# One load of w3 is issued as five: 96 partitions and four times 8 partitions

## The chip, the cores and the metric

The kernel runs on one core of one Trainium2 chip. The metric is device time in microseconds (us): the median of three runs is 822.88 us before the change, and the three lie between 820.26 and 823.59 us.

The core has five engines, each with an instruction stream of its own that it works through in order: PE (matrix multiplication, with its weight loads shown as PEld), DVE (VectorE), ACT (ScalarE), POOL (GpSimd) and SP (SyncE). In this kernel SP issues the DMA transfers. Engines wait for one another, and for transfers, on semaphores.

## The reference, cut to what matters

Three parts follow one another: attention with a window of 128 positions, a gated product layer, and a layer with a squared ReLU.

```python
scores = scale * np.matmul(q, k.transpose(0, 1, 3, 2))      # 4 x 8 heads, 576 x 64
scores = np.where(mask, scores + bias[None], -1000000000.0) # 0 <= rel < 128
attn = softmax(scores)
x = np.matmul(attn, v)                                      # -> 2304 x 512
h = (x @ w1) * (x @ w2) @ w3                                # w3: 1024 x 1024
x = h @ w_out                                               # 1024 x 512
h = np.maximum(x @ w_in, 0.0)
out = h * h @ w_out2
```

The weights come as 64-bit floating point numbers. The kernel reads them as pairs of 32-bit words and makes 32-bit numbers of them on ACT and DVE.

## The kernel before, in words

**Stages.** The first 150 us or so are attention, worked in 16 pairs of heads. For a pair, two loads (L393, one a head, 64 partitions each) bring q and k into one tile `qk`, of which there are two; four loads (L398, L402, L406, L407) bring v. PE makes the scores (L467) from `qk`, DVE adds the bias and takes a minimum (L435), ACT takes the exponential (L443), PE transposes (L503), ACT or DVE copies the transposes (`pt`, L200), and PE multiplies with v (L527, L543). The first 64 rows of `qk` belong to the pair's first head and the last 64 to its second, so the first matmul of a pair needs the first of its two loads, and the second matmul needs the second one.

**What lies between.** In the gaps of attention the kernel loads weights and multiplies w3 by w_out (L659), which is needed from the first product layer on. w3 comes in 8 blocks, `("w3", 0)` to `("w3", 7)`, each of 128 partitions x 8192 bytes, by `w_load`; w_out comes in 4 such blocks, also by `w_load`. Each block is then made into 32-bit numbers by three instructions: `conv_s` (L339 when on DVE), `conv_g` (ACT, L330) and `conv_m` (DVE, L345). The later stages (L195 to L197, L1080 to L1082, L1131 to L1133) are long rows of matmuls.

**What sets the order.** The class `Plan` simulates the engines with a cost for each task and writes one fixed order for each engine's instructions before the kernel is built. A load task such as `ldw30` has one cost, whatever number of DMA instructions `w_load` issues for it. SP issues all loads and stores in the planned order, one after the other, and an issue that waits holds up all that stand behind it.

**Eight semaphores for the transfers.** The framework gives the transfers eight semaphores in turn, DMAHW0 to DMAHW7. From the ninth transfer on, each issue first waits until the transfer that had the same semaphore, the eighth before it, has landed. Beside that an issue waits for the engine that still reads the tile it will overwrite.

The function `w_load` issues the load of a w3 block in one line:

```python
nc.sync.dma_start(out=t.rearrange("p n w -> p (n w)"), in_=src[i].bitcast(U32))
```

Of the kernel before, what the change touches and what calls it, by code (L numbers as in the profile page):

```python
# [9 lines left out]
U32 = mybir.dt.uint32  # L10
# [16 lines left out]
MK = 0  # L27
NKEEP = 3
OM = 5
OB = 1  # L30


# [120 lines left out]
def fused_kernel(  # L153
# [11 lines left out]
    nc = tc.nc  # L165
# [46 lines left out]
    m_scr = {(k, m): dram.tile([128, 1024], F32, name=f"m_scr{k}{m}") for k in "ic" for m in range(NM)}  # L212
    m_scr.update({("o", m): dram.tile([128, 1024], F32, name=f"m_scro{m}") for m in (*range(OM, NM), *range(OM))})

# [97 lines left out]
    def w_load(key):  # L312
        kind, i = key
        src = {"wo": w_out, "w3": w3t, "w12": w12}[kind]
        if kind == "wo":
            t = su.tile([128, 1024, 2], U32, tag="v", bufs=4, name="raw")
        else:
            t = wp.tile([128, 1024, 2], U32, tag="u", bufs=11, name="raw")
        if kind == "wo":
            nc.sync.dma_start(  # L320
                out=t.rearrange("p (c n) w -> p c (n w)", c=2),
                in_=src[i * 256:(i + 1) * 256, :].bitcast(U32).rearrange("(c p) n -> p c n", p=128),
            )
        else:
            nc.sync.dma_start(out=t.rearrange("p n w -> p (n w)"), in_=src[i].bitcast(U32))
        raws[key] = t

    def conv_g(key):
# [32 lines left out]
    def add_words(key, rank, tag, users, keep, lead):  # L361
        k = "%s%d" % key
        hold("raw" + k, tag, users)
        add("ld" + k, rank - lead, {"dma": w_dma(1048)}, lambda e: w_load(key), takes=["raw" + k], keep=keep)
        add("cg" + k, rank, w_act(1024), lambda e: conv_g(key), ["ld" + k])
        add("cs" + k, rank, w_ts(1024, "Da"), lambda e: conv_s(key, e), ["ld" + k])
        add("cn" + k, rank, {"D": 1.16}, lambda e: conv_m(key, flat(raws[key])), ["cg" + k, "cs" + k])
# [1068 lines left out]
    for x, (k, m) in enumerate([k for k in m_scr if k[0] != "c"]):  # L1436
        if (k, m) == ("o", OM):
            prev = prev + [f"wlbc{FO[OB][-1]}{OB}"]
        if (k, m) == ("o", 0):
# [84 lines left out]
```

## Time and profile before

| What | Value |
|---|---|
| median of three runs | 822.88 us (820.26 to 823.59) |
| the profiled execution's own time | 819.97 us |
| its span, first to last instruction | 818.1 us |
| PE busy | 803.4 us, 98% of the span |
| DVE, ACT, POOL busy | 75%, 57%, 7% |
| moved by DMA | 144.01 MB in 98403 packets |
| granted TensorE clock | 1.000 of full speed |

The profile divides the span into 40 slices and gives each engine's busy share in tenths. The trace can be asked for the instructions of a stretch in order of time, for what ended an engine's idle time, for the busy time in chosen stretches, and for the DMA issues with the time from issue to landing. A row "SPq" is an issue of a transfer: its length is the time SP took to issue it, not the transfer.

### The profile page before, as it was taken

To read this page: it belongs to the slowest core of one execution; us is meant where nothing else is said; L and a number is where in the kernel's file an instruction comes from. 1 tells how busy PE (TensorE), PEld (TensorE's weight loads), DVE (VectorE), ACT (ScalarE), POOL (GpSimd) and SP (SyncE) were. 2 spreads that over 40 slices of the span, in tenths; PEclk is the share of its full clock that TensorE was granted. 3 is DMA by queue.
4 is the path that set the end of the run, shared out by engine and by line. 5 is a ranking of instruction groups with operands and counts; after the bars stand their busy time and mean duration, and the time that the engine had idled before them with its cause. 6 is when DMAs were issued, how large, how long until landed. Compare 5 with 4: busy or idle time off the path is not lost. (4 is left out here: it accounts for less than half of the span.)

```text
span 818.1 us, 17284 instructions
## 1 busy us (share of the span) xinstructions
PE 803.4 (98%) x6732; PEld 747.6 (91%) x6732; DVE 613.3 (75%) x1361; ACT 466.7 (57%) x1006; POOL 57.5 (7%) x69
## 2 busy tenths in 40 slices
PE   7999999999999999999999999999999999999998
PEld 6666566599999899999999999999999999999998
DVE  6999899966798996896499475733766897667762
ACT  6999978633233452341344476755786776666631
POOL 1000000000001000110040130000221100000000
PEclk9999999999999999999999999999999999999999
DMA  9989898698623643202133457765773745544201
GB/s 232 295 260 296 287 291 238 252 318 279 224 84 107 207 162 94 67 11 89 39 109 108 159 185 253 240 225 210 237 246 136 216 145 162 151 141 139 87 27 34
DMA packets 98403, 144.01 MB, mean 176 GB/s; under 512 B 11024, under 2 KB 75024, under 8 KB 96272
## 3 DMA queue, kind: packets, MB, share of 16 engines
q1 hardware_dynamic: 98320, 142.90, 55.2%
q8 instruction: 53, 0.87, 0.4%
q14 instruction: 30, 0.25, 0.1%
HBM read 98.44 MB, written 44.43 MB: 175 GB/s over the span
## 5 line engine op out<-in xcount | busy, mean ns | idle before, releaser
L196 PE MATMUL g<-gt,wu 128*128 128x288 f32 x256 | 75.7, 296 | 0.0
L195 PE MATMUL g<-gt,wu 128*128 128x288 f32 x256 | 75.6, 295 | 0.0
L197 PE MATMUL g<-gt,wu 128*128 128x288 f32 x256 | 75.4, 295 | 0.0
L443 ACT ACTIVATE e<-e,st 128x192 f32<-128x192 f32 (+1 forms) x144 | 62.4, 436 | 9.8 <-DVE st L435 9.2
L659 PE MATMUL g<-raw 128*128 128x512 f32 x128 | 62.4, 602 | 0.0
L200 ACT ACTIVATE D<-xa 128x384 f32<-128x384 f32 (+1 forms) x99 | 44.9, 453 | 29.3 <-PE xa L1133 23.8
L1192 DVE TENSOR_TENSOR D<-xb,D 128x384 f32<-128x384 f32 (+1 forms) x62 | 32.2, 520 | 37.8 <-PE xb L1133 18.0
L1080 PE MATMUL al<-x,wc 128*128 128x288 f32 x192 | 57.5, 299 | 1.1 <-ACT d L200 1.1
L1082 PE MATMUL al<-x,wc 128*128 128x288 f32 x192 | 56.7, 295 | 0.0
L1081 PE MATMUL al<-x,wc 128*128 128x288 f32 x192 | 56.5, 294 | 0.0
L203 DVE TENSOR_TENSOR ww<-fq,ww 128x1024 fp32r<-128x1024 f32 x35 | 42.5, 1222 | 16.8 <-ACT ww L200 16.5
L200 ACT ACTIVATE ye<-g 128x288 f32<-128x288 f32 x32 | 13.1, 410 | 72.9 <-PE g L197 65.6
L200 ACT ACTIVATE ww<-fq 128x1024 fp32r<-128x1024 f32 x35 | 36.9, 1056 | 27.9 <-PE xb L1133 12.2
L1264 ACT ACTIVATE D<-D 128x384 f32<-128x384 f32 x73 | 37.5, 521 | 23.5 <-DVE D L1192 22.4
L196 PEld LDWEIGHTS g<-gt,wu 128*128 128x128 f32 x256 | 48.3, 189 | 0.0
L197 PEld LDWEIGHTS g<-gt,wu 128*128 128x128 f32 x256 | 48.2, 188 | 0.0
L868 DVE TENSOR_TENSOR st<-st 128x256 f32<-128x256 f32 (+1 forms) x105 | 41.0, 425 | 9.5 <-DMA st<-m_scrc 5.7
L195 PEld LDWEIGHTS g<-gt,wu 128*128 128x128 f32 x256 | 48.1, 188 | 0.0
L200 ACT ACTIVATE d<-al 128x288 f32<-128x288 f32 x71 | 28.7, 409 | 32.2 <-PE al L1082 22.9
L503 PEld LDWEIGHTS t<-ident,e 128*128 128x128 f32 x208 | 23.6, 140 | 22.9 <-ACT pt L200 10.3
L435 DVE CUSTOM_DVE_ANT_0 e<-s,bw 128x192 f32<-128x192 f32 (+1 forms) x128 | 40.6, 351 | 2.5 <-PE s L467 2.1
L467 PE MATMUL s<-qk 64*64 64x128 f32 (+2 forms) x768 | 36.9, 281 | 4.6 <-DMA qk<-in_qk_dram 3.2
(284 smaller groups left out, 2780.8 us busy)
## 6 DMA issues: line engine op xcount, KB each, us to landing
s_scr<-D SPq DMA_DIRECT2D x96, 192.0 KB, 2.1
u<-in_w2io_dram SPq DMA_DIRECT2D x32, 512.0 KB, 6.8
fo<-s_scr SPq DMA_DIRECT2D x20, 512.0 KB, 5.1
qk<-in_qk_dram SPq DMA_DIRECT2D x32, 288.0 KB, 4.9
st<-m_scrc SPq DMA_DIRECT2D x18, 512.0 KB, 3.7
raw<-in_w3t_dram SPq DMA_DIRECT2D x8, 1024.0 KB, 7.3
raw<-in_w_dram SPq DMA_DIRECT2D x8, 1024.0 KB, 7.6
fq<-s_scr SPq DMA_DIRECT2D x16, 512.0 KB, 5.2
```

The lines of the kernel that those rows point to most:

```text
L195: nc.tensor.matmul(o, wh, xh, start=start, stop=False)
L196: nc.tensor.matmul(o, wh, xl, start=False, stop=False)
L197: nc.tensor.matmul(o, wl, xh, start=False, stop=stop)
L200: nc.scalar.activation(out=o, in_=i, func=ACTF.Copy)
L203: eng.tensor_tensor(out=o, in0=a, in1=b, op=ALU.subtract)
L435: nc.vector.tensor_tensor_reduce(out=part_of(m, x, rows), in0=ps, in1=bias, op0=ALU.add, op1=ALU.min, scale=-0.125, scalar=3.0e38, accum_o ...
L443: nc.scalar.activation(out=e, in_=e, func=ACTF.Exp, bias=st[:, 0, x:x + 1], scale=-1.0, accum_out=st[:, 1, x:x + 1],)
L659: nc.tensor.matmul(gw[fi], wl, wr, start=c == 0, stop=c == 7)
L868: ENG[e].tensor_tensor(out=o, in0=a, in1=b, op=op)
L1080: nc.tensor.matmul(o, wh, xh, start=start and c == 0, stop=False, skip_group_check=True)
L1081: nc.tensor.matmul(o, wh, xl, start=False, stop=False, skip_group_check=True)
L1082: nc.tensor.matmul(o, wl, xh, start=False, stop=c == 1, skip_group_check=True)
```

## The change

The first block of w3 is loaded by five DMA instructions: partitions 0 to 95, then 96 to 103, 104 to 111, 112 to 119 and 120 to 127. The bytes and the place they go to stay. All other loads keep one instruction.

```diff
 OM = 5
+APART = (("w3", 0),)
 OB = 1
...
         else:
-            nc.sync.dma_start(out=t.rearrange("p n w -> p (n w)"), in_=src[i].bitcast(U32))
+            cut = (0, 96, 104, 112, 120, 128) if key in APART else (0, 128)
+            for a, b in zip(cut, cut[1:]):
+                nc.sync.dma_start(out=t[a:b].rearrange("p n w -> p (n w)"), in_=src[i, a:b].bitcast(U32))
         raws[key] = t
```

The orders of PE, DVE, ACT and POOL stay as they are; SP has four more issues. On SP, from the second pair's v loads to the third pair's v loads, this stood before (`raw` is a weight block as loaded, the semaphores each issue waits for stand in brackets):

```order
L398 DMA v_167<-in_v_main_dram 128x2x256 [waits DMAHW0_49]
L402 DMA v_167<-in_v_main_dram 64x2x128 [waits DMAHW1_49]
L406 DMA v_167<-in_v_main_dram 64x2x64 [waits DMAHW2_49]
L407 DMA v_167<-in_v_rest_dram 64x2x64 [waits DMAHW3_49]
L325 DMA raw<-in_w3t_dram 128x2048 [waits DMAHW4_49]
L393 DMA qk<-in_qk_dram 64x2x576 [waits DMAHW5_49,PE_49]
L393 DMA qk<-in_qk_dram 64x2x576 [waits DMAHW6_49]
L393 DMA qk<-in_qk_dram 64x2x576 [waits DMAHW7_49,PE_49]
L393 DMA qk<-in_qk_dram 64x2x576 [waits DMAHW0_49]
L320 DMA raw<-in_w_out_dram 128x2x1024 [waits DMAHW1_49]
L325 DMA raw<-in_w3t_dram 128x2048 [waits DMAHW2_49]
L398 DMA v_166<-in_v_main_dram 128x2x256 [waits DMAHW3_49,PE_49]
```

Now, from the block of w3 on, the same stretch of SP reads:

```order
L328 DMA raw<-in_w3t_dram 96x2048 [waits DMAHW4_49]
L328 DMA raw<-in_w3t_dram 8x2048 [waits DMAHW5_49]
L328 DMA raw<-in_w3t_dram 8x2048 [waits DMAHW6_49]
L328 DMA raw<-in_w3t_dram 8x2048 [waits DMAHW7_49]
L328 DMA raw<-in_w3t_dram 8x2048 [waits DMAHW0_49]
L396 DMA qk<-in_qk_dram 64x2x576 [waits DMAHW1_49,PE_49]
L396 DMA qk<-in_qk_dram 64x2x576 [waits DMAHW2_49]
L396 DMA qk<-in_qk_dram 64x2x576 [waits DMAHW3_49,PE_49]
L396 DMA qk<-in_qk_dram 64x2x576 [waits DMAHW4_49]
L321 DMA raw<-in_w_out_dram 128x2x1024 [waits DMAHW5_49]
L328 DMA raw<-in_w3t_dram 128x2048 [waits DMAHW6_49]
L401 DMA v_166<-in_v_main_dram 128x2x256 [waits DMAHW7_49,PE_49]
```

Four issues stand between the first piece of the block and the next `qk` load, and each later transfer has the semaphore four further on. The four loads of `qk` wait for the four v loads of the pair before and for the 96-partition piece, where they waited for earlier transfers; the load of w_out and the next w3 block wait for the first two small pieces. On PE, the first matmuls of the third pair stood so before (`s` is a bank of scores, `qk_286` the pair's tile):

```order
L569 MATMUL g_347<-ident_119 128x128 x2
L467 MATMUL s_350<-qk_286 64x128 [waits DMAHW5_49,DVE_49]
L467 MATMUL s_351<-qk_286 64x128 [waits DMAHW6_49,DVE_49]
L467 MATMUL s_350<-qk_286 64x128
L467 MATMUL s_351<-qk_286 64x128
```

and now:

```order
L572 MATMUL g_351<-ident_119 128x128 x2
L470 MATMUL s_354<-qk_290 64x128 [waits DMAHW1_49,DVE_49]
L470 MATMUL s_355<-qk_290 64x128 [waits DMAHW2_49,DVE_49]
L470 MATMUL s_354<-qk_290 64x128
L470 MATMUL s_355<-qk_290 64x128
```

The instructions are the same; only the semaphores of the two `qk` loads have moved, with their transfers. The first reader of the w3 block on DVE waits for five transfers instead of one. It was, and is:

```order
L339 TENSOR_SCALAR raw<-raw 128x1024 [waits DMAHW4_49]
```

```order
L342 TENSOR_SCALAR raw<-raw 128x1024 [waits DMAHW6_49,DMAHW5_49,DMAHW7_49,DMAHW4_49,DMAHW0_49]
```

It stands at the same place in DVE's order. Source lines after the change are three higher, from `w_load`'s loop on.

## Rows read from the trace of the kernel before

**Rows 1.** The page: busy time of the engines, and shares by slice.
```profile
PE 803.4 (98%) x6732; PEld 747.6 (91%) x6732; DVE 613.3 (75%) x1361; ACT 466.7 (57%) x1006; POOL 57.5 (7%) x69
...
PE   7999999999999999999999999999999999999998
...
PEclk9999999999999999999999999999999999999999
```

**Rows 2.** Busy time by stretch; after the counts: granted clock, DMA share, GB/s.
```profile
10.00:20.00 10.00, 7.61 (x115) 6.01 (x117) 8.25 (x47) 8.67 (x33) 0.00 (x0) 1.00 1.04 280
20.00:30.00 10.00, 9.30 (x192) 7.25 (x187) 9.71 (x50) 9.56 (x36) 0.00 (x0) 1.00 0.96 302
...
80.00:100.00 20.00, 20.00 (x212) 11.94 (x211) 17.02 (x62) 18.53 (x57) 0.00 (x0) 1.00 0.88 295
```

**Rows 3.** What PE waited for in 0 to 160 us: in total, times, longest.
```profile
PE s L467 <- DMA qk<-in_qk_dram: 3.2, 4, 1.0
PE t L503 <- ACT pt L200: 2.2, 4, 1.0
...
PE s L467 <- DVE raw L339: 0.9, 1, 0.9
```

**Rows 4.** Timeline, 16.6 to 19.5 us: start, length, instruction, idle before and its end.
```profile
16.70 0.43 PE L467 MATMUL s<-qk 64*64 64x128 f32 x2
...
16.95 0.36 DVE L435 CUSTOM_DVE_ANT_0 e<-s,bw 64x192 f32<-64x192 f32 x1
...
17.35 0.69 DVE L339 TENSOR_SCALAR raw<-raw 128x1024 uint32<-128x1024 uint32 x1
...
18.06 1.10 PE L467 MATMUL s<-qk 64*64 64x128 f32 x30 [0.93 <-DVE raw L339]
...
19.46 0.29 DVE L435 CUSTOM_DVE_ANT_0 e<-s,bz 128x128 f32<-128x128 f32 x1 [1.42 <-PE t L503]
```

**Rows 5.** The DMA issues on SP, from 8.61 us on.
```profile
8.61 0.59 SPq L325 DMA_DIRECT2D raw<-in_w3t_dram  x1
...
10.03 0.61 SPq L393 DMA_DIRECT2D qk<-in_qk_dram  x1
...
13.96 0.59 SPq L393 DMA_DIRECT2D qk<-in_qk_dram  x1
...
14.60 1.45 SPq L393 DMA_DIRECT2D qk<-in_qk_dram  x1
16.10 0.60 SPq L320 DMA_DIRECT2D raw<-in_w_out_dram  x1
```

**Rows 6.** Issues at 6.04, 8.61 and 10.03 us: size, time to landing.
```profile
v<-in_v_main_dram SPq DMA_DIRECT2D x1, 256.0 KB, 5.3
...
raw<-in_w3t_dram SPq DMA_DIRECT2D x1, 1024.0 KB, 6.0
...
qk<-in_qk_dram SPq DMA_DIRECT2D x1, 288.0 KB, 7.9
```

**Rows 7.** DMA from 11.2 to 12.8 us, where packets of 8 KB alone run.
```profile
DMA packets 77, 0.63 MB, mean 394 GB/s; under 512 B 0, under 2 KB 0, under 8 KB 0
...
q1 hardware_dynamic: 77, 0.63, 96.7%
```

**Rows 8.** The page: all packets, and those that fetch instructions.
```profile
DMA packets 98403, 144.01 MB, mean 176 GB/s; under 512 B 11024, under 2 KB 75024, under 8 KB 96272
...
q8 instruction: 53, 0.87, 0.4%
```

**Rows 9.** DMA from 14 to 15.7 us: the queue that fetches instructions.
```profile
q8 instruction: 1, 0.02, 4.9%
```

**Rows 10.** Timeline of PE at 66 and at 143 us.
```profile
67.37 0.94 PE L467 MATMUL s<-qk 64*64 64x128 f32 x23 [1.01 <-DMA qk<-in_qk_dram]
...
143.74 0.56 PE L467 MATMUL s<-qk 64*64 64x128 f32 x8 [0.84 <-DMA qk<-in_qk_dram]
```

## The prediction

> **What bounds the kernel now.** I read the page first. PE is busy 803.4 us of the 818.1 us span, nine tenths or more in all slices but the first and at the full granted clock throughout [rows 1]. So the span is PE's work plus some 15 us in which PE waits, and a change to a load can act only through those waits. The windows show where they are: 7.61 of 10 us busy in 10 to 20 us, 9.30 in 20 to 30 us, all 20.00 in 80 to 100 us [rows 2]. Next I asked what ended PE's waits in attention: three things, `qk` loads (3.2 us, 4 times), ACT's copies of transposes (2.2 us), and once 0.9 us put down to DVE's L339 [rows 3]. The last deserves distrust. The timeline has the third pair's first score matmul at 16.70 us (a pair of records) and the other 15 (30 records) only at 18.06 us, after 0.93 us idle [rows 4]. In the order on PE the second of these matmuls waits for the second `qk` load of the pair and for DVE; what it needs of DVE is a score bank that L435 has read, and the last L435 before it ended at 16.95 + 0.36 = 17.31 us [rows 4]. The second `qk` load was issued at 10.03 us [rows 5] and took 7.9 us to land [rows 6], at 17.93 us. That landing is what PE waits for; L339 ends beside it by coincidence (17.35 + 0.69 = 18.04 us). This `qk` load is the first thing that SP issues behind the block of w3, so the change acts on it. DVE waits for PE there in turn (1.42 us until 19.46 us, [rows 4]), so it isn't a stall that DVE would have had anyway.
>
> **The change part by part.**
>
> *SP.* Four issues are added. The issue of a block takes 0.59 us and of a `qk` load 0.59 to 0.61 us [rows 5]. No issue of 8 partitions is in the trace, so I bound it from nothing to 0.64 us (an issue and the gap to the next, as from 13.96 to 14.60 us, [rows 5]) and take 0.64: the issues vary little though sizes vary by far. Four make 2.6 us. After the second `qk` load SP stands idle from 10.64 to 13.96 us, 3.32 us [rows 5], because the next load waits for PE to release its tile. The 2.6 us fit into that.
>
> *Waits on the semaphores.* The fourth small piece now waits for the second pair's first v load, which was issued at 6.04 us and landed 5.3 us later [rows 6], at 11.3 us; the pieces before it reach SP at 9.25, 9.9 and 10.5 us and their predecessors have landed. The small pieces are therefore out at about 12.0 us, the two `qk` loads at 12.0 to 12.6 and 12.6 to 13.3 us, 2.6 us later than before and still 0.7 us ahead of 13.96 us. Behind the waiting piece only `qk` loads are queued. The next load of w_out waits for the first small piece, and the next w3 block for the second; these will have landed by about 15 us (below), and SP comes to them at 16.10 us now. Price: nothing, and if the cover goes, as much as the sum exceeds 3.32 us.
>
> *A stall of SP.* The issue at 14.60 us takes 1.45 us instead of 0.6 [rows 5], and in that stretch one packet runs on the queue that fetches instructions [rows 9]; there are 53 of these in the whole program [rows 8]. With four more issues ahead SP reaches the same place of its stream four issues earlier, at the last small piece. Then the `qk` loads go out 0.85 us later again, at up to 14.1 us: a cost of 0 to 0.85 us. I take 0 since the engines have other bytes to work on until then.
>
> *The transfer itself.* Between 11.2 and 12.8 us nothing but packets of 8 KB run, at 394 GB/s with the sixteen engines 96.7% busy [rows 7]: a packet takes 8192 B / (394 GB/s / 16) = 0.33 us of one engine. A row of w3 is one such packet (the 16 blocks of 128 rows, 2048, and the 53 fetches account for nearly all of the 98403 - 96272 = 2131 packets of 8 KB or more, [rows 8]). Now each engine gets 8 rows. Then 96 rows are 6 for each, and a piece of 8 rows can occupy 8 engines at most. If the four pieces go to different halves in turn, every engine has 8 rows again: 0. If all four go to the same eight, these have 10 rows and the others 6: 2 x 0.33 = +0.67 us on the one half, -0.67 us on the other. If each piece goes to a single engine, and all to the same, that one has 32 rows more in place of two: 30 x 0.33 = +9.9 us. The rows nearest to it, the sixteen engines evenly at work on a block, speak for spreading a piece as far as its rows go, and nothing alternates in a rule that looks at one transfer at a time: I take +0.67 us.
>
> The Trainium skill, "DMA: Bandwidth & Descriptors", section "Why a DMA increments its semaphore by 16 and not by 1", says that a transfer runs on the largest number of engines up to 16 that divides the slowest dimension of both sides, and names the lowest-numbered ones. By it 96 rows run on all engines and each piece of 8 on the same eight, which would again be +0.67 us and speaks against the change; no piece of 8 partitions is in this trace to show it. The same page's "Rules for kernel authors" holds that two transfers to disjoint halves serialize and aren't worth having; by that alone the sum is 0.
>
> *Who is late.* The block itself is read first by DVE at 17.35 us [rows 4]; it lands at 8.61 + 6.0 = 14.6 us [rows 5, 6]. A landing at 15.3 us, or 16.1 with the stall of SP, leaves over a microsecond. The engines take the `qk` rows after the block's, so the second `qk` load lands when the more loaded half is through: 17.93 + 0.67 = 18.6 us. DVE's L339 is then done, and PE's wait of 0.93 us grows to 1.6 us. From 20 to 30 us DVE and ACT are over 95% busy [rows 2] on what PE feeds them, so nothing close behind takes it back.
>
> *Sum.* +0.67 us on the path. On the profiled execution: 819.97 + 0.67 = 820.6 us (818.8 of span and 1.9 around it). That execution lies 2.9 us below the median of the three runs, so against the median: 822.88 + 0.67 = 823.5 us. Bounds of this course: 0 and +1.5 us (with SP's stall).
>
> **The rivals.**
>
> *Nothing moves (822.9 us).* The load that is last is so on one engine, and if that engine is in the half with 6 rows, its gain cancels the other half's loss; or the pieces spread evenly. For it: 7.9 us to land for a `qk` load against 6.0 for a block three times its size and issued before it [rows 6] says that the load is held by what is ahead of it on the engines, not by its issue. Against it: the half with more rows carries a full 0.67 us.
>
> *Faster (821.4 us).* With the fetches of instructions four issues further ahead in the order, SP's stalls of 0.85 us fall elsewhere. Two more waits of PE end with a `qk` load, 1.01 us before 67.37 us and 0.84 us before 143.74 us [rows 10]; a load that is issued 0.85 us sooner could take away most of each. Both: -1.7, and with the +0.67 near -1; with the even case -1.5, which I take. Were every microsecond of these two and of the 0.93 us at 18 us gone, it would be -2.8 us, 820.1 us. Against it: the DMA engines are full in attention (a share of 0.88 to 1.04, [rows 2]), so an earlier issue mostly waits in their queues; and the stalls can as well fall on a load that is on time now.
>
> *Slower (833 us).* A piece of 8 rows goes to one engine, the same for all four. That engine has 38 rows; the `qk` rows behind them come 9.9 us later, and PE stands at the third pair until 18.06 + 9.9 = 28 us, with DVE and ACT waiting for its scores. Price +9.9 us: 832.8 us. It decides as soon as PE's wait of 0.93 us grows beyond 0.93 + 4.1 = 5.0 us, that is from 4.1 / 0.33 = 12 rows too many on one engine. Against it: a block's 128 packets do spread evenly [rows 7], and 8 rows can be divided as 128 can.
>
> *The change doesn't do what it says:* SP's order shows five issues, so it does.
>
> **How the numbers follow.** Forecast +0.67 us: 0.55. Nothing: 0.25. Faster by 1 to 2.8 us: 0.15. Slower by 9.9 us: 0.05. A measurement of this kernel can tell about 0.5%, 4.1 us, from no change (the three runs lie 3.3 us apart). The first three all lie inside it. For the faster side beyond 4.1 us no mechanism reaches; I leave 0.05 to the spread of runs on top of the third case. For the slower side 0.05 from the fourth and 0.02 from spread: 0.07. The rest is 0.88. The range: from 820.1 us (the bound of the faster case, also near the lowest run) to 823.5 + 0.85 (SP's stall) + 1.7 (half the distance between the three runs) = 826.0 us.
>
> **What would show it.** Five issues on SP where one was, the fifth ending near 12 us and the two `qk` loads by 13.3 us; the next pair of `qk` loads still at about 14 us, released by PE. The second `qk` load lands at 18.6 us and PE's wait before the rest of the third pair's scores is about 1.6 us; PE's busy time stays at 803 us, and the waits at 66 and 143 us stay within 1 us of what they are. Wrong would be: the block's reader on DVE waiting for a piece; PE's wait at 18 us unchanged or shorter, which would mean that the last engine is in the lighter half or the pieces spread; a wait of several microseconds there, which would mean that a piece runs on few engines; a fall of the granted clock after it.

## The result, and the profile after

| | Before | After |
|---|---|---|
| median of 20 runs each | 820.76 us (818.82 to 824.22) | 824.78 us (823.3 to 834.27) |
| ratio | 1 | 1.0054, interval 1.0036 to 1.0072 |
| the profiled execution: its own time, its span | 819.97, 818.1 us | 824.66, 822.8 us |
| mean granted TensorE clock | 1.000 | 0.994 |

The change makes the kernel 0.54% slower, 4.0 us. The forecast was +0.67 us. The 824.78 us lie inside the range 820.1 to 826.0 us, but partly because the range was built on a median of three runs, 822.88 us, and over 20 runs the kernel before is 2.1 us faster than that. That is luck: added to the median of 20 runs, the same upper bound is 820.76 + 0.67 + 0.85 + 1.7 = 824.0 us, and 824.78 lies above it. The mechanism was the right one, a later `qk` load for the third pair; its size was not.

The page of the kernel after, engines and granted clock, answers to [rows 1]:

```profile
PE 804.7 (98%) x6732; PEld 749.6 (91%) x6732; DVE 613.9 (75%) x1361; ACT 466.6 (57%) x1006; POOL 57.0 (7%) x69
...
PEclk9899999999999999999999999999999999999999
```

PE is busy 1.3 us longer and the span is 4.7 us longer, so PE also stands 3.4 us more. The clock's digit in the second slice, 21 to 41 us, is 8 and no longer 9. PE's waits in 0 to 160 us of the kernel after, to set beside [rows 3]:

```profile
PE s L470 <- DMA qk<-in_qk_dram: 7.0, 4, 4.0
PE t L506 <- ACT pt L201: 2.5, 4, 1.0
```

Waits on `qk` have grown to 7.0 us, with one of 4.0. The timeline of PE after shows that one, where [rows 4] has the scores of the third pair:

```profile
16.32 0.61 PE L572 MATMUL g<-ident 128*128 128x128 f32 x4
20.97 0.66 PE L470 MATMUL s<-qk 64*64 64x128 f32 x2 [4.04 <-DMA qk<-in_qk_dram]
23.01 0.69 PE L470 MATMUL s<-qk 64*64 64x128 f32 x7 [1.39 <-DMA qk<-in_qk_dram]
```

The first matmul of the pair runs at 20.97 us instead of 16.70, the others from 23.01 instead of 18.06: both `qk` loads are late, the second by 4.95 us, and the wait of 0.93 us became 5.43 us. DVE waits too, for the block itself:

```profile
19.64 0.70 DVE L342 TENSOR_SCALAR raw<-raw 128x1024 uint32<-128x1024 uint32 x1 [2.16 <-DMA raw<-in_w3t_dram]
```

The block's first reader starts at 19.64 us instead of 17.35 [rows 4], when the last small piece has landed. PE isn't held up by it, since its scores come later still. The issues on SP after, beside [rows 5]:

```profile
8.63 2.99 SPq L328 DMA_DIRECT2D raw<-in_w3t_dram  x5
11.88 4.59 SPq L396 DMA_DIRECT2D qk<-in_qk_dram  x4
```

SP has issued the five pieces by 11.62 us, and the `qk` loads follow at once, as forecast. They go out 2.5 us later than before (11.88 against 9.39 us); an experiment below shows that this alone costs nothing. What each kernel moves is shown by the DMA rows of one microsecond, 12 to 13 us, in which packets of 8 KB alone run. The kernel before:

```profile
DMA packets 54, 0.44 MB, mean 442 GB/s; under 512 B 0, under 2 KB 0, under 8 KB 0
```

The kernel after, the same microsecond:

```profile
DMA packets 27, 0.22 MB, mean 221 GB/s; under 512 B 0, under 2 KB 0, under 8 KB 0
```

Half the packets: the 96 rows move at half the rate of the 128 rows. When the small pieces run beside the `qk` loads, the whole core moves less still, 15.1 to 16.6 us after:

```profile
DMA packets 94, 0.26 MB, mean 174 GB/s; under 512 B 24, under 2 KB 24, under 8 KB 77
```

The 17 packets that are not under 8 KB are rows of the small pieces. In the trace such rows take 0.65 to 1.17 us each, where a row of the undivided block took 0.31 us. Behind them, 17 to 19 us after:

```profile
DMA packets 94, 0.19 MB, mean 93 GB/s; under 512 B 13, under 2 KB 13, under 8 KB 94
...
q1 hardware_dynamic: 94, 0.19, 91.9%
```

Here no packet of 8 KB starts any more; what runs are rows of `qk` loads. The sixteen engines are 92% busy and move 93 GB/s, some 0.36 us for each of the 81 rows (2 us x 16 x 0.92 / 81, an estimate). In the kernel before, such a row took 0.16 us in the median of 13 to 18 us.

The trace also records each increment of a transfer's semaphore. Each small piece ends with eight of them, and the pieces end one after another, at 16.49, 17.41, 18.74 and 19.62 us. Of the sixteen increments of the third pair's first `qk` load, seven come by 16.8 us and nine from 19.3 to 20.8 us; before, all sixteen came from 15.3 to 15.9 us. So the four pieces stand behind one another on about half of the engines, as the prediction took it, and the `qk` rows behind them wait there.

While PE waits, its clock falls; the windows of the kernel after, beside [rows 2]:

```profile
10.00:20.00 10.00, 5.17 (x68) 4.05 (x68) 7.54 (x44) 8.37 (x33) 0.00 (x0) 0.93 1.05 194
20.00:30.00 10.00, 7.65 (x109) 6.11 (x110) 4.84 (x23) 4.07 (x12) 0.00 (x0) 0.56 0.95 269
```

The last two fields but one are the granted clock and the DMA share. The clock is 0.93 of full in 10 to 20 us and 0.56 in 20 to 30 us, that is, mostly at the lower of its two levels, 1.2 instead of 2.4 GHz; it fell within the 4.04 us in which PE stood idle, until 20.97 us. DVE and ACT are half idle there, 4.84 and 4.07 of 10 us busy instead of 9.71 and 9.56.

How the loss travels shows in the first start and the last start of two groups, before:

```profile
L659 PE MATMUL g<-raw x128: 592/592/697, 37.8 to 163.8; 128*128 128x512 f32 x128
...
L1080 PE MATMUL al<-x,wc x192: 288/296/402, 228.9 to 429.4; 128*128 128x288 f32 x192
```

and after:

```profile
L662 PE MATMUL g<-raw x128: 592/592/697, 44.3 to 169.1; 128*128 128x512 f32 x128
...
L1083 PE MATMUL al<-x,wc x192: 288/296/404, 233.6 to 434.2; 128*128 128x288 f32 x192
```

The matmul that started at 37.8 us is now 6.5 us late: 4.95 us were there at the third pair's second matmul, and 1.55 us more came behind it, in the stretch at the lower clock. The one that started at 228.9 us is 4.7 us late, and it stays so. In between the kernel won some of it back. No wait on a `qk` load behind the third pair is left in the kernel after, so both waits of [rows 10] are gone. But matmul by matmul the kernel is 6.3 us late up to the first of them, 5.6 us behind it, and 6.3 again from 78 us on, where later scores start late. Behind the second, at 143 us, it is 5.3 us late, and from 181 us on 4.7; what gave the last 0.5 us was not followed.

### The profile page after: what moved, and what is told of

It reads as the page before. It is cut to its first block, busy times and chain, and to the rows that moved or that the text cites. A ratio compares the mean times of both kernels' runs of the same rounds, so it can differ in the third digit from the quotient of the medians.

```text
span 822.8 us, 17292 instructions
## 1 busy us (share of the span) xinstructions
PE 804.7 (98%) x6732; PEld 749.6 (91%) x6732; DVE 613.9 (75%) x1361; ACT 466.6 (57%) x1006; POOL 57.0 (7%) x69
## 5 line engine op out<-in xcount | busy, mean ns | idle before, releaser
L201 ACT ACTIVATE ye<-g 128x288 f32<-128x288 f32 x32 | 13.1, 409 | 73.4 <-PE g L198 66.0
L470 PE MATMUL s<-qk 64*64 64x128 f32 (+2 forms) x768 | 37.8, 288 | 7.8 <-DMA qk<-in_qk_dram 7.0
L470 PEld LDWEIGHTS s<-qk 64*64 64x64 f32 x768 | 28.1, 136 | 17.0 <-issue 8.1
```

The lines of the kernel that those rows point to most:

```text
L201: nc.scalar.activation(out=o, in_=i, func=ACTF.Copy)
L470: nc.tensor.matmul(HD[2 * m + r]["s"][g][o, c:c + w], t[h, 0, 64 * q:64 * q + 64], t[h, 1, 64 * k:64 * k + w], start=True, stop=True,)
```

## The experiments

Three theories: A, the issues and semaphore waits of SP make the loss; B, the two rows more on eight engines, as forecast; C, a piece that covers a part of the partitions moves each row more slowly. The measured times:

| Kernel | Median, us | Ratio to before, interval | PE's waits for the third pair's `qk`, us |
|---|---|---|---|
| changed kernel | 824.78 | 1.0054 (1.0036 to 1.0072) | 4.04 + 1.39 |
| four tiny transfers instead | 820.22 | 0.9997 (0.9977 to 1.0017) | 0.82 |
| 96 + 32 partitions | 823.52 | 1.0036 (1.0022 to 1.005) | 0.93 + 2.06 |
| halves | 824.86 | 1.0054 (1.0037 to 1.0072) | 0.99 + 1.91 |
| even and odd partitions | 821.92 | 1.0015 (1.0000 to 1.0029) | 0.35 |
| seven pieces over all partitions | 821.02 | 1.001 (0.9998 to 1.0022) | 0.99 + 0.86 |
| changed, PE kept at work | 824.07 | 1.0051 (1.0033 to 1.007) | 0.23 |
| changed, small pieces behind `qk` | 827.68 | 1.0097 (1.0079 to 1.0115) | 0.62 (DVE) + 1.81 |
| before, one `qk` load a pair | 816.28 | 0.995 (0.9935 to 0.9964) | none |
| the same, and one v load a pair | 816.11 | 0.9941 (0.9925 to 0.9957) | none |
| one `qk` load, with the change | 818.84 | 0.9973 (0.996 to 0.9986) | 2.21 |

**SP's share alone.**

```diff
 nc.sync.dma_start(out=t.rearrange("p n w -> p (n w)"), in_=src[i].bitcast(U32))
+if key == ("w3", 0):
+    for x in range(4):
+        s = dram.tile([8, 4], F32, name=f"tiny{x}")
+        nc.sync.dma_start(out=s, in_=qk[0, 0, 0, 8 * x:8 * x + 8, 0:4])
```

> The block of w3 is one load of 128 partitions again, followed by four more transfers of 8 rows x 16 bytes from one DRAM place to another, which nothing reads. SP thus has the changed kernel's issues and its waits on the eight semaphores, without its way of moving the block. Theory A (the issues and waits of SP make the loss): the second qk load of the third pair lands near 22 us as in the changed kernel, PE waits 4 to 5 us there, the time is 3 to 5 us above the kernel before. Theory B (the extra rows on eight engines) and theory C (a piece that covers a part of the partitions moves each row more slowly) both expect: 8 KB packets of 0.31 to 0.33 us, that load landed at 18 to 18.5 us, PE's wait there 0.9 to 1.4 us, no fall of the clock, the time within 1 us of the kernel before.

Nothing is lost, the ratio is 0.9997. On PE of this kernel the third pair starts where it did:

```profile
16.84 0.40 PE L471 MATMUL s<-qk 64*64 64x128 f32 x2
18.06 1.10 PE L471 MATMUL s<-qk 64*64 64x128 f32 x30 [0.82 <-DMA qk<-in_qk_dram]
```

Theory A falls: four more issues and the semaphores four places on cost nothing, as the prediction had it. Its `qk` loads were even issued later than in the changed kernel (from 12.16 instead of 11.88 us). Tiny transfers land soon, so this kernel has no issue that waits for a slow piece. In the changed kernel three do, for 1.0, 0.3 and 1.0 us, but they stand behind the third pair's `qk` loads, and SP then waits 9.8 us more for PE.

**Two pieces, every engine with 8 rows.** With 96 + 32:

```diff
+cuts = (slice(0, 96), slice(96, 128)) if key == ("w3", 0) else (slice(0, 128),)
+for c in cuts:
+    nc.sync.dma_start(out=t[c].rearrange("p n w -> p (n w)"), in_=src[i, c].bitcast(U32))
```

> The block in two pieces, 96 and 32 partitions, so that every engine has 8 rows again (6 + 2). Theory B (two rows more on eight engines): as the kernel before, the second qk load of the third pair landed at 18 us, PE's wait 0.9 us, time within 1 us. Theory C (a piece of part of the partitions is slow): the 96 rows at 0.56 us a packet as in the changed kernel, the 32 rows at least as slow, so 8 x 0.56 = 4.5 us or more for the block instead of 2.7 to 3.3 us; that load lands at 19.5 us or later, PE waits over 2 us there, time +1.5 to +4 us. Theory A (issues): one issue more, as the kernel before.

PE in the kernel with 96 + 32:

```profile
17.69 0.40 PE L469 MATMUL s<-qk 64*64 64x128 f32 x2 [0.93 <-DMA qk<-in_qk_dram]
20.14 1.98 PE L469 MATMUL s<-qk 64*64 64x128 f32 x30 [2.06 <-DMA qk<-in_qk_dram]
```

Its 96 rows run at 229 GB/s in 12 to 13 us. By the prediction's count there is no uneven share of rows here, and yet two thirds of the loss are there (0.36 of 0.54%). Theory B isn't enough, theory C holds. Next the halves, `cuts = (slice(0, 64), slice(64, 128))`:

> The block in two halves, partitions 0 to 63 and 64 to 127. Theories A and B: 8 rows on every engine and one issue more, as the kernel before within 1 us. Theory C: 8 KB packets of 0.5 to 0.6 us (a qk load of 64 partitions moves 2304 B in 0.15 to 0.17 us, which is 14 to 15 GB/s of one engine, and 8192 B at that rate are 0.55 us); the block takes 4.4 us instead of 2.7 to 3.3 us, the second qk load of the third pair lands at 19 to 20 us, PE waits 2 to 3 us there, time +1 to +2 us, more if the clock falls.

DMA, 12 to 13 us, with the halves:

```profile
DMA packets 32, 0.23 MB, mean 229 GB/s; under 512 B 4, under 2 KB 4, under 8 KB 4
```

Half rate, PE's waits are 2.90 us, as theory C said. The time is 4.1 us above before, more than the +1 to +2 us expected; the clock fell (0.83 in 20 to 30 us), for which the expectation had left room. Then the same two pieces of 64 rows, taken by even and odd partitions:

```diff
-cuts = (slice(0, 64), slice(64, 128)) if key == ("w3", 0) else (slice(0, 128),)
+cuts = (slice(0, 128, 2), slice(1, 128, 2)) if key == ("w3", 0) else (slice(0, 128),)
```

> The block in two pieces of 64 partitions, the even ones and the odd ones, so that each piece reaches over all 128. If in theory C what counts is the number of rows in a piece, this is as the two halves: packets of 0.5 to 0.6 us, that qk load at 19 to 20 us. If what counts is the stretch of partitions that a piece covers, packets take 0.31 to 0.33 us, the load lands at 18 to 18.5 us and the time is within 1 us of the kernel before. Theories A and B: as the kernel before.

DMA, 12 to 13 us, with even and odd partitions:

```profile
DMA packets 69, 0.43 MB, mean 434 GB/s; under 512 B 16, under 2 KB 16, under 8 KB 16
```

Full rate. The number of rows and of pieces is the same as with the halves; only which partitions go together differs. So the stretch of partitions counts, and not the count of rows. The time is 1.2 us above before, just outside the 1 us expected; the ratio, 1.0015 with an interval from 1.0000, leaves at most a small loss.

**Which side, SBUF or DRAM.** Two loads of 64 rows, where a host layout of the block lets one side be a contiguous half and the other every second row. Written to every second partition, read from a contiguous half (`out=t[x:128:2]`, `in_=src[i, 64 * x:64 * x + 64]`):

> The block in two loads of 64 rows: each reads 64 rows that follow one another in DRAM (the block was laid out so) and writes to every second partition. If the stretch of partitions that is written counts, 8 KB packets take 0.31 us as with the even and odd halves, and the second qk load of the third pair lands at 18 us. If the stretch of DRAM that is read counts, packets take 0.55 to 0.63 us as with the two halves, and that load lands at 20 us or later.

DMA, 12 to 13 us:

```profile
DMA packets 67, 0.42 MB, mean 418 GB/s; under 512 B 16, under 2 KB 16, under 8 KB 16
```

And the reverse (`out=t[64 * x:64 * x + 64]`, `in_=src[i, x:128:2]`):

> The reverse: each of two loads reads every second row of the block in DRAM and writes 64 partitions that follow one another. If the partitions written count: packets of 0.55 to 0.63 us and that qk load at 20 us or later. If the stretch of DRAM counts: 0.31 us and 18 us.

DMA, 12 to 13 us:

```profile
DMA packets 38, 0.22 MB, mean 221 GB/s; under 512 B 11, under 2 KB 11, under 8 KB 11
```

The partitions that are written decide, and the stretch of DRAM that is read doesn't. Each was run once (820.4 and 823.14 us), so the rates carry this, not the times. PE's waits agree: none for the third pair's `qk` loads in the first, 1.17 + 2.07 us in the second.

**The forecast's own term.** Seven pieces, all reaching over the whole tile, with the row counts of the changed kernel (the small pieces hold 32 rows together):

```diff
+cut = [slice(x, 128, 4) for x in range(3)] + [slice(x, 128, 16) for x in (3, 7, 11, 15)]
+for c in cut:
+    nc.sync.dma_start(out=t[c].rearrange("p n w -> p (n w)"), in_=src[i, c].bitcast(U32))
```

> The block in seven pieces that each reach over all partitions: three of 32 rows (every fourth partition) and four of 8 rows (every sixteenth). The eight engines that take the small pieces have 10 rows, the others 6, as in the changed kernel. Theory B alone (two rows too many at 0.33 us): 8 KB packets of 0.31 to 0.33 us, the second qk load of the third pair lands at 18.5 to 19 us, PE's wait there is 1.4 to 2 us, time +0.5 to +2 us over the kernel before. If a piece of 8 rows is slow by itself, wherever its rows lie: packets of 0.7 us and more for these, that load at 20 us or later, time +3 to +5 us. If neither counts: landed at 18 us, time within 1 us of before.

PE with the seven pieces:

```profile
17.83 0.40 PE L470 MATMUL s<-qk 64*64 64x128 f32 x2 [0.99 <-DMA qk<-in_qk_dram]
19.09 1.90 PE L470 MATMUL s<-qk 64*64 64x128 f32 x30 [0.86 <-DMA qk<-in_qk_dram]
```

The second matmul starts 1.03 us later than before (19.09 against 18.06) and 1.07 us later than with even and odd partitions (18.02), with packets of 0.31 us up to 13 us. That is near theory B's 0.67 us, but it can't be put down to it. SP's seven issues keep the `qk` loads back until 13.24 us, and the DMA share, the last field but one, falls meanwhile:

```profile
8.64 4.47 SPq L328 DMA_DIRECT2D raw<-in_w3t_dram  x7
13.24 2.34 SPq L396 DMA_DIRECT2D qk<-in_qk_dram  x3
...
13.00:14.00 1.00, 1.00 (x19) 0.60 (x17) 0.96 (x5) 0.87 (x4) 0.00 (x0) 1.00 0.64 197
14.00:15.00 1.00, 0.73 (x6) 0.45 (x4) 1.00 (x7) 0.72 (x3) 0.00 (x0) 1.00 0.49 123
```

The sixteen DMA engines are half idle before the `qk` rows come, and the sixteen increments of the first `qk` load lie together, from 16.5 to 17.7 us. So the late issue explains the delay as well, and two rows too many at the full rate show no cost of their own here: from nothing to about 1 us. Pieces of 8 rows aren't slow wherever their rows lie: between 13 and 15 us, where mostly such rows run, a row takes 0.3 to 0.5 us and not 0.7 or more. The time, +0.1%, can't be told from before.

**The clock.** The changed kernel with matmuls of no use in PE's two waits:

```diff
+for x, a in enumerate(todo):
+    if (m, g) == (2, 0) and x < 2:
+        p_warm("g", (17, 6)[x])
+    mm(*a)
```

> The changed kernel, with 17 and 6 matmuls of the identity on itself (128 columns, result not used) on PE ahead of the first and the second score matmul of the third pair, where PE stood idle 4.04 and 1.39 us. The loads are as in the changed kernel, so PE's scores come as late. If the fall of the granted clock (half speed from 18.5 to 28.7 us) is a part of the loss: the clock stays at full speed, ACT and DVE are some 5 us late at 24 us instead of 7.2 us, and the time is 1.5 to 2.5 us below the changed kernel (822.3 to 823.3 us). If the late loads alone make the loss and the fall costs nothing, the time is that of the changed kernel, 824 to 825.5 us.

Windows of this kernel:

```profile
20.00:30.00 10.00, 9.08 (x145) 7.22 (x148) 5.96 (x30) 5.94 (x20) 0.00 (x0) 1.00 0.99 281
```

The third pair's second matmul, and the two groups of matmuls followed above, in this kernel:

```profile
22.56 1.10 PE L470 MATMUL s<-qk 64*64 64x128 f32 x30 [0.23 <-DMA qk<-in_qk_dram]
...
L664 PE MATMUL g<-raw x128: 592/592/697, 42.3 to 168.1; 128*128 128x512 f32 x128
...
L1085 PE MATMUL al<-x,wc x192: 288/296/402, 232.6 to 433.1; 128*128 128x288 f32 x192
```

The clock stays at full speed, and the group that began at 44.3 us begins at 42.3. Of these 2.0 us, 0.45 were there at the pair's second matmul (22.56 against 23.01). This kernel is 4.5 us behind the kernel before there and still 4.5 us at the group's start, so the 1.55 us that the changed kernel lost in between were the clock's, in these traces. At the end of the second group 1.1 us of the 2.0 are left (433.1 against 434.2). The time, 824.07 us, isn't in the expected 822.3 to 823.3, and its ratio can't be told from the changed kernel's. So a part of the clock in the loss is seen in one trace of each, and its size in the time is open: nothing to about 2 us.

**The small pieces behind the `qk` loads.** The diff leaves `cut = (0, 96)` in `w_load` and issues the four pieces after the third pair's second load:

```diff
+if n == 5:
+    for a in range(96, 128, 8):
+        nc.sync.dma_start(out=raws["w3", 0][a:a + 8].rearrange("p n w -> p (n w)"), in_=w3t[0, a:a + 8].bitcast(U32))
```

> The changed kernel, with the four pieces of 8 partitions issued behind the two qk loads of the third pair instead of ahead of them. Theory C: the 96 rows take as long at 0.56 us each as the 128 rows did, so the second qk load lands at 17.5 to 18.5 us, PE waits 0.5 to 1.5 us there, the clock stays, and the time is within 1.5 us of the kernel before although all five pieces are there. If the split costs by something other than these qk loads (its bytes on eight engines, the semaphores, SP's stream), the time stays at 824 to 825.5 us.

This expectation failed: it is the slowest kernel of all. DVE shows why:

```profile
23.87 0.69 DVE L342 TENSOR_SCALAR raw<-raw 128x1024 uint32<-128x1024 uint32 x1 [6.55 <-issue]
24.59 0.29 DVE L441 CUSTOM_DVE_ANT_0 e<-s,bz 128x128 f32<-128x128 f32 x1
```

The block's reader, which started at 17.35 us before, now waits 6.55 us, with the score work behind it. The view names no releaser; the reader waits for all five pieces, and the last of them landed at 23.7 us. The second `qk` load is late with only the 96 rows ahead of it (the matmul at 19.61 us instead of 18.06), though the small pieces queued behind may have a part in that. The small pieces are slow in both places (0.6 to 1.4 us a row here); the place only chooses who waits.

**A faster version.** If a stretch of 64 partitions halves the rate, the `qk` loads are themselves slow: each fills a half of the tile. Laid out on the host by pairs, one load fills it all:

```diff
     if n % 2 == 0:
         PR[n // 2]["qk"] = at.tile([128, 2, S], F32, tag="qk", bufs=2, name="qk")
-    r = 64 * (n % 2)
-    nc.sync.dma_start(out=PR[n // 2]["qk"][r:r + 64], in_=qk[b, h].rearrange("t d s -> d t s"))
+        nc.sync.dma_start(out=PR[n // 2]["qk"], in_=qk[b, h // 2])
...
-"qk": c(_np.stack([q, k], axis=2).transpose(0, 1, 2, 4, 3)),
+"qk": c(_np.stack([q, k], axis=2).transpose(0, 1, 4, 2, 3)).reshape(B, H // 2, 128, 2, S),
```

> The kernel before, with q and k of a pair of heads laid out so that one load of 128 partitions x 4608 bytes brings them, in place of two of 64 x 2 x 2304 bytes. If a load on a stretch of 64 partitions runs at about half rate (0.15 to 0.17 us for 2304 bytes), one load of all 128 runs at the rate of the w_out loads (4096 bytes in 0.16 us): 4608 bytes in about 0.19 us. PE's waits on qk loads (0.49, 0.83, 0.93, 1.01 and 0.84 us in the kernel before) shrink or vanish, time 2 to 4 us below before. If the size of the packets or the number of transfers made the qk loads slow, packets of 4608 bytes take 0.3 us, the waits stay, and the time is as before; the first pair starts later, as its first matmul then waits for all of the pair.

What PE waited for in the whole program of this kernel:

```profile
PE t L502 <- ACT pt L200: 2.7, 6, 1.0
PE be L1079 <- DVE d L1102: 1.7, 2, 1.3
```

No wait on a `qk` load is left, the third pair runs at 16.55 us without one, and the time is 816.28 us, 0.5% below before. In the trace the rows of 4608 bytes take 0.18 us in the median, near the 0.19 us expected from the stretch of partitions and not the 0.3 us of the other case. This beats both kernels. The same for v, whose four loads (`L398` to `L407`) become `nc.sync.dma_start(out=v.rearrange("p h c d -> p (h c d)"), in_=v_all[b, p])` on a host layout that holds the six blocks of v side by side:

> The kernel with one qk load for a pair, and v of a pair also laid out so that one load of 128 partitions x 3072 bytes takes the place of four, three of which cover 64 partitions (48 issues fewer on SP). If loads of half of the partitions and their small packets still hold back attention: 1 to 2 us below the kernel with one qk load. If PE no longer waits for loads there (its trace has no wait on qk left), the same time within 1 us. Slower only if the first pair's matmuls come later.

816.11 us: the same within what can be told. With PE's waits on `qk` gone, faster v loads buy nothing here. And the change itself, the five pieces of the first w3 block, on the kernel with one `qk` load:

> The change made on the kernel with one qk load for a pair. Theory C: the 96 rows (0.56 us each) and the small pieces (0.7 us and more) hold the same engines as before, so the third pair's qk load lands at 18 to 20 us where it landed at 14.4 us, PE waits 1 to 3 us there that it did not, time +1.5 to +4 us over the kernel with one qk load. If the loss came only with qk loads that are themselves slow, the time stays within 1 us of it.

```profile
18.72 1.11 PE L468 MATMUL s<-qk 64*64 64x128 f32 x32 [2.21 <-DMA qk<-in_qk_dram]
```

That row is PE's third pair; it waits 2.21 us that it did not, and the ratios to before are 0.9973 with the change and 0.995 without it (818.84 and 816.28 us, from separate sets of runs, whose intervals just touch). So the loss needs no slow `qk` load behind the pieces.

## Why the prediction was right in kind and wrong in size

- *What bounds the kernel, and where the change acts:* right. The wait put down to L339 was the second `qk` load's, and that load moved.
- *SP:* right. 0.27 to 0.6 us an issue; the fourth small piece left at 11.35 us, where 11.3 was worked out, and the `qk` loads were issued by 13.1 us. The tiny transfers show that this costs nothing. The stall of SP did not show at the last small piece.
- *Waits on the semaphores:* the price of nothing held for the third pair, its reason did not. The first two small pieces landed at 16.49 and 17.41 us and not by 15 us, and SP waited 1.0 us for the 96 rows before the fourth pair's second `qk` load and 0.3 us for a small piece before the next w3 block, both behind the loads that PE waited for.
- *The transfer itself:* this step failed. "A packet takes 0.33 us of one engine" was read from a load of all 128 partitions and used for rows of 96 and of 8. In 12 to 13 us the 96 rows run at 221 GB/s instead of 442, 0.55 us a row, and the rows of the small pieces take 0.65 to 1.17 us. The term of +0.67 us measured +4.95 us at the second `qk` load. The choice of "the same eight" engines fits the semaphores; what was mis-sized is the time of a row. With 96 + 32 rows the second matmul is 2.08 us late (20.14 against 18.06); the other 2.9 us came with cutting the last 32 rows into four. How these divide into rows too many on one half and slower rows isn't shown: at the full rate the seven pieces leave nothing to 1 us for the first. The profile before held the sign of it: the `qk` loads of 64 partitions took 7.9 us to land where a block over three times their size took 6.0 [rows 6], which I put down to the queue alone, and a row of theirs moved at 14 to 15 GB/s of one engine, where a row of the block had about 25 (8192 B in 0.33 us).
- *The bounds:* 0 and +9.9 us held the term, but I treated the upper one as a rival for one engine and gave it 0.05. A course between the two, slow pieces on several engines, had no place of its own. That the time lay in the range is luck in part, as said above.
- *Who is late, and what follows:* the wait was to be 1.6 us and was 5.43. The block was to land by 15.3 us with over a microsecond to spare; its last piece landed at 19.6, and DVE's reader waited 2.16 us for it, which the prediction had named as a sign of being wrong. A fall of the clock was named as a sign of a wait of several microseconds, and came; no price was put on it.
- *"Nothing close behind takes it back":* right, the kernel is 6.3 us late up to 66 us. Of the 1.8 us won back later about 1 us came at the second of the two waits that the faster rival had named; what the first gave was lost again by 78 us.

The Trainium skill, "DMA: Bandwidth & Descriptors", "Rules for kernel authors", says that two transfers to disjoint halves of the partitions serialize and share the same engines, and advises a single one. The halves agree with the advice and show more than that: 229 GB/s instead of 442, while the even and the odd partitions, also disjoint and also two transfers, ran at 434 GB/s.

The cause inside the chip stays open. That each group of partitions has a limited way in would fit the halves; but 96 partitions ran no faster (213 to 246 GB/s in four kernels) than 64 (221 and 229 GB/s). A limit for each group does not explain that without more, and no run shows which engine writes which partition.

## What to carry to other kernels

Read a load's rate from a load over the same partitions: here a contiguous 64 or 96 of the 128 ran at half the rate of all, and a step of 2 over all of them ran at the full one. Before a load is cut, look at what stands behind it in the queue, since a slow piece holds the engines for whoever comes next; moving it here only changed who waits. A wait of a few microseconds on PE may cost more than itself (1.55 us more here, in the traces), so look at the granted clock in it and behind it.

## What the runs showed of the hardware that I had not expected

- In 12 to 13 us, packets of 8 KB from one DRAM block moved at 410 to 442 GB/s when they were written to all partitions or to every second one, and at 213 to 246 GB/s when written to a contiguous 64 or 96. For the 64 the order in DRAM made no difference.
- Rows of pieces of 8 partitions took 0.65 to 1.17 us beside `qk` loads (174 GB/s in all), and the `qk` rows right behind them held the sixteen engines 92% busy at 93 GB/s.
- With PE's waits of 0.99 and 1.91 us (halves) the granted clock in 20 to 30 us was 0.83, with 4.04 and 1.39 us (the change) it was 0.56, and with PE kept at work through them 1.00.
